# Packed attention with two expert layers on one core: urgencies from backward plans, and six units without moves within SBUF

## The chip, the cores and the metric

One core of one Trainium2 chip runs one launch. The time is device microseconds (us) from one execution; a kernel's time is the median of its runs. TensorE (PE) multiplies, VectorE (DVE), ScalarE (ACT) and GpSimd (POOL) work on vectors, and SyncE (SP) issues nearly all DMAs. On-chip data lies in SBUF; products come out in banks of PSUM.

## The reference

There are 8 batches of 8 heads, 576 positions, 64 elements a head, and 32 packed positions. All is float32 (the weights are laid out as 64-bit floats).

```
p_packed = softmax(p k^T / 8) v          # 32 x 64 a head
att      = softmax(q p_packed^T / 8) p_packed
x   = att as 4608 x 512
h   = x w_in;  s = h softmax(h);  x = layernorm(s) g_ln w_out     # 512 -> 1024 -> 512
out = relu(x moe2_w_in)^2 moe2_w_out                              # 512 -> 2048 -> 512
```

## The kernel before

The kernel writes no instruction at once. Each step is entered in a plan (`plan.op`, `plan.either`) with an engine or several, an estimated duration, an urgency, and the tiles that it reads and writes. `Plan.order` then simulates the five queues (TensorE, ScalarE, GpSimd, VectorE, and one for DMAs): whenever an engine is free it takes the ready step of least urgency number. `Plan.emit` writes the instructions in the order so found, and each engine executes its own in that order. A step waits in its engine's queue until its semaphores come, and all behind it waits too. DMAs are issued from SP in the order of the plan.

**Urgencies.** They are hand-set times: a unit of attention gets `att_at(n)`, with the constants `QA`, `GA`, `UN` and others for single steps; a tile of the first expert layer gets `T0 + DT * i`, and so on for weights and the second layer.

**Attention.** There are 16 units of four heads (`pack` and `unpack`), two to a batch. `pack` loads k (`kr`) and q (`qr`), transposes them on VectorE in blocks of 32 into `kT` (L537, L540) and `qT` (L548), computes the first scores (`s1`), their maximum (`mx`, `nmx`), exp (`e1`, L575), its transposes on TensorE (L588), the packed values (`ppp`, L602; `pp`, L608), and their transposes into `ppq`. `unpack` computes the second scores (`s2`) from `ppq` and q, transposes them (`a`, L637), does the softmax over 32 positions on VectorE, GpSimd and ScalarE, and leaves `aT`; it also multiplies the packed values by w_in (`pg`, L648) into the tile `G`. Line L373 issues the DMAs, L386 is the rounded copy of `hi_op`, L389 the subtraction of `lo_op`.

The scores of a unit contract over 64 elements of each head. In the transposed layout the elements lie in two halves `e` of 32 across four heads. The function `pairs` moves a transposed tile by four DMAs within SBUF (`k2`, `q2`), so that two heads stand in 128 partitions with whole contractions; `pair_mm` (L478) then makes two products of 64 columns of the array each. An `early` unit (n < `NK`, which is 4) does this for q but not for k: its first scores contract the two halves one after the other over the whole array (L560) with the operand `pb`, in which each head has its own columns.

**Buffers.** A ring of n buffers gives the tile n places earlier in the same ring to the next one, after all its uses. k and q share the ring `raw` (`RAW` = 1), `kT`, `qT` and `e1` the ring `tmp` (2), `pr`, `pp` and (other units) `pT` the ring `s` (2), in the order in which they are entered in the plan.

**The first expert layer.** Its tiles of 128 tokens (`h_tile`, 36 of them) need `G` and `aT` of both units of a batch; from the second batch on each operand is split into a high and a low part (`ah`, `al`), the low one by a subtraction (`ALO` names the engine). After softmax and layer norm the tile is transposed (`ptv`) and multiplied by w_out (`y_stage`, `py`). `decode` turns the 64-bit weights into float32; `SIN` and `SOUT` say which engine restores the signs of w_in and w_out (L422 and L423 on VectorE, or L426 and L428 on ScalarE with L430 on VectorE). The second layer (`z_group`, `o_products`) follows and computes seven products of blocks where eight would be plain.

Of the kernel before, what the change touches and what calls it, by code (L numbers as in the profile page):

```python
# [90 lines left out]
class Plan:  # L91

    WINDOW = 3413.0

    @staticmethod
# [21 lines left out]
    def either(self, engines, urgency, fn, r=(), w=(), lag=0, claim=(), port=False):  # L120
# [24 lines left out]
        deps.discard(i)  # L145
        self.ops.append(Op(engines, urgency, fn, lag, bufs, deps, port))

    def order(self):
        ops = self.ops
        users = [[] for _ in ops]  # L150
        left = [len(o.deps) for o in ops]
        able = [[] for _ in range(5)]
# [39 lines left out]
        def take(e, t):  # L192
            nonlocal port
            while not busy[e] and able[e]:
                _, i = heapq.heappop(able[e])
                o = ops[i]
                if o.engine is not None:
                    continue
                o.engine = e
                busy[e] = True  # L200
                order.append(i)
                if e == POOL or e == DVE and o.port:
                    port = self.span = max(t, port) + o.engines[e]
                else:
                    self.span = pe_end(t, o.engines[e]) if e == PE else t + o.engines[e]
                heapq.heappush(events, (self.span, i, "free"))
                heapq.heappush(events, (self.span + o.lag, i, "done"))

# [25 lines left out]
        assert len(order) == len(ops), "the plan is stuck"  # L234
        return order

    def emit(self):
        with self.tc.manual_schedule():
            for i in self.order():
                self.ops[i].fn(self.ops[i].engine)  # L240
            for s in reversed(list(self.stacks.values())):
                s.close()
# [3 lines left out]
def kernel(  # L246
# [36 lines left out]
    KJ = (S + P - 1) // P  # L283
    SH = S // 2
    ST = 256
    AB, GB, RAW, TMP, VR, ET = 4, 4, 1, 2, 1, 1
    QA, GA, HA, TR, UN = 55.91, 149.84, 34.68, -39.93, -11.33
    NK = 4
    WD, WDS, WIS = 99.51, 175.52, 17.0
    GSC = (POOL,)  # L290
    SIN, SOUT = DVE, ACT
    GX = 1
    SUB, KLO, ALO = (POOL,), (DVE,), (DVE,)
    ZSIN, OSIN = DVE, DVE
    SN, FN, LATE = 5.72, -26.79, 3090.0
    YB, ZL, OL, GL0, GL1, GL2, PS, CS = 197.3, 148.71, 20.73, 15.29, 13.31, 32.6, 1.04, 186.23
    NST = NT // ST
    HN = 384
    NSZ = NT // (2 * HN)
# [58 lines left out]
    def c_prod(n, cols, whole):  # L358
        return c_mm(n * (4 if whole else 3), cols, whole)

    def c_dve(cols, fast=False):
        return 66 + (0.525 if fast else 1.045) * cols
# [107 lines left out]
    rows = [min(P, S - j * P) for j in range(KJ)]  # L470

    pbz = [ab.tile([P, 2, HG, 32] if i == 0 else [P, 2, 2, 32], F32, f"pbz{i}") for i in range(3)]
    PAIR = 4 * (0.4336 * SH + 6)

    def pair_mm(ps, lhs, rhs, cs):

        for e in range(2):
            nc.tensor.matmul(ps()[64 * e:64 * e + 64, :SH], cols(lhs, e), cols(rhs, e)[:, cs], start=True, stop=True)  # L478
# [13 lines left out]
    def pack(at, b, g):  # L492
# [43 lines left out]
        for e in range(2):  # L536
# [10 lines left out]
        qT = ab.tile([P, 2, NB, T], F32, "qT", tag="tmp", bufs=TMP)  # L547
        plan.op(DVE, c_dve(2 * S), at + QA, lambda: nc.vector.transpose(  # L548
            out=qT().rearrange("p e n t -> p n e t"), in_=qr().rearrange("p n (e i) -> p n e i", e=2)), r=[qr], w=[qT])
        qs = pairs(at + QA + 1, qT, "q2")  # L550

        mx = ab.tile([P, 2], F32, "mx")
        s1 = []
# [44 lines left out]
        def pp_mm():  # L598
            for j in range(KJ):
                m = rows[j]  # L600
                for e in range(2):
                    nc.tensor.matmul(  # L602
                        ppp()[64 * e:64 * e + 64, :2 * D].rearrange("p (h m i) -> p h m i", h=2, m=2),
                        eT()[:m, j, 64 * e:64 * e + 64], vr()[:m, 2 * e:2 * e + 2, j, :].rearrange("p m (h i) -> p h m i", h=2), start=j == 0, stop=j == KJ - 1)
        plan.op(PE, KJ * 267, at + 10, pp_mm, r=[eT, vr], w=[ppp])

        pp = ab.tile([P, 2, P], F32, "pp", tag="s", bufs=2)
        plan.op(DVE, c_dve(256) + 60, at + 12, lambda: nc.vector.scalar_tensor_tensor(  # L608
# [7 lines left out]
        def pp_tr():  # L616
            for e in range(2):
# [2 lines left out]
        ppq = ab.tile([P, 2, 64], F32, "ppq", bufs=2)  # L620
        hi_op(at + 12, P, ppq,
              lambda: ptp()[:, :2 * (P + 64)].rearrange("p (e n) -> p e n", e=2)[:, :, :64], [ptp], [ppq])
        return ppq, qs

    g_tiles, a_tiles = {}, {}

    def unpack(at, b, g, packed):
        ppq, qs = packed

        a = ab.tile([P, NB, NP], F32, "a1", bufs=1)  # L630
        for hf in range(2):
            s2 = bank("s2")

            def s2_mm(s2=s2, cs=slice(hf * SH, (hf + 1) * SH)):
                pair_mm(s2, ppq, qs, cs)
            plan.op(PE, PAIR, at, s2_mm, r=[ppq, qs], w=[s2])
            plan.op(DVE, c_dve(SH), at + 1, lambda s2=s2, bs=slice(hf * NB // 2, (hf + 1) * NB // 2): nc.vector.transpose(  # L637
                out=a()[:, bs, :], in_=s2()[:, :SH].rearrange("p (n t) -> p n t", t=T)), r=[s2], w=[a])

        gt = m1.tile([P, 1, F1], F32, "G", bufs=GB) if b < GX else m1.tile([P, 2, F1], F32R, "G", bufs=GB)  # L640
        for f in range(F1 // 512):
            pg = bank("pg")
            fs = slice(f * 512, (f + 1) * 512)

            def g_mm(pg=pg, fs=fs):
                for e in range(2):
                    es = slice(64 * e, 64 * e + 64)
                    nc.tensor.matmul(pg()[es, :], ppq()[:, e], wi[2 * g + e]()[:, fs], start=True, stop=True)  # L648
            plan.op(PE, 885, at + GA, g_mm, r=[ppq, wi[2 * g], wi[2 * g + 1]], w=[pg], claim=[gt])
            hi_op(at + GA + 1, 512, lambda fs=fs: gt()[:, 0, fs], pg, [pg], [gt])  # L650
            if b >= GX:
                lo_op(at + GA + 1, 512, lambda fs=fs: gt()[:, 1, fs], pg, lambda fs=fs: gt()[:, 0, fs], [pg, gt], [gt], (DVE,))
        g_tiles[b, g] = gt
        m2_ = ab.tile([P, NB], F32, "m2_")
        plan.op(DVE, c_dve(S), at + 2, lambda: nc.vector.tensor_reduce(
            out=m2_(), in_=a(), axis=AX.X, op=ALU.max), r=[a], w=[m2_])
        plan.either({e: on(S, e)[e] if e == DVE else 1110 for e in SUB}, at + 3, lambda e: vec[e].tensor_tensor(
            a(), a(), m2_().unsqueeze(2).to_broadcast([P, NB, NP]), op=ALU.subtract), r=[a, m2_], w=[a])
        plan.op(ACT, c_act(S, sbuf=True), at + 4, lambda: nc.scalar.activation(a(), a(), AF.Exp, scale=scale), r=[a], w=[a])
        d2 = ab.tile([P, NB], F32, "d2")  # L660
        plan.op(DVE, c_dve(S), at + 5, lambda: nc.vector.tensor_reduce(
            out=d2(), in_=a(), axis=AX.X, op=ALU.add), r=[a], w=[d2])
        plan.op(DVE, 85, at + 5, lambda: nc.vector.tensor_scalar(d2(), d2(), 1e-9, None, op0=ALU.add), r=[d2], w=[d2])
        plan.op(DVE, 180, at + 5, lambda: nc.vector.reciprocal(d2(), d2()), r=[d2], w=[d2])
        plan.op(POOL, 1110, at + 6, lambda: nc.gpsimd.tensor_tensor(
            a(), a(), d2().unsqueeze(2).to_broadcast([P, NB, NP]), op=ALU.mult), r=[a, d2], w=[a])
        aT = m1.tile([P, NB, T], F32, "aT", bufs=AB)
        plan.op(DVE, c_dve(S), at + 7, lambda: nc.vector.transpose(out=aT(), in_=a()), r=[a], w=[aT])
        a_tiles[b, g] = aT
# [144 lines left out]
    g_mark = [[[plan.mark("g") for _ in range(4)] for b in range(4)] for st in range(NSZ)]  # L814


    T0, DT = 127.57, 23.948
    PD0, PD = 111.2, 23.139
    UD, UA, U1 = 25.541, 213.28, -45.68
    WI, WO, WOD, YL = 162.35, 266.68, 65.988, 3.36  # L820
    units = [(b, g) for b in range(B) for g in range(NG)]
    att_at = lambda n: U1 * n if n < NG else T0 - UA + UD * (n - NG)
    packed = {}
# [332 lines left out]
            o_products(at, st)  # L1156

    second()
    plan.emit()


# [28 lines left out]
```

## Time and profile before

| | us |
|---|---|
| median of 3 runs (lowest, highest) | 1263.37 (1262.45, 1266.02) |
| profiled execution | 1262.49 |
| its span, first to last instruction | 1260.4 |
| TensorE busy in the span | 1205.5 |
| VectorE, ScalarE, GpSimd busy | 906.0, 789.7, 171.7 |

A share of busy time over the span is a mean over stages with different limits, so the stages have to be looked at one by one. Matmuls overlap, and their ends are modelled in the profile: of two neighbours the distance of their starts tells more than the duration.

### The profile page before, as it was taken

What the parts mean: (1) busy time and instruction counts of PE and PEld (TensorE: products, weight loads), DVE (VectorE), ACT (ScalarE), POOL (GpSimd) and SP (SyncE); (2) the same over time, 40 slices, a digit from 0 to 9 for tenths busy, and PEclk for the clock granted to TensorE, in tenths of its full rate; (3) what the DMA queues carried; (4) which work ended last, traced back from release to release, by engine and by line L of the source; (5) the groups of instructions that cost most, each with busy time, mean ns of one, the idle gap of its engine ahead of it and who ended that gap; (6) DMA issues with size and microseconds to landing.
All of it is one profiled execution on the core that took longest, in us unless ns stands there. A gap on an engine that the chain in (4) does not pass through costs nothing.

```text
span 1260.4 us, 23326 instructions
## 1 busy us (share of the span) xinstructions
PE 1205.5 (96%) x8332; PEld 1101.2 (87%) x8332; DVE 906.0 (72%) x1817; ACT 789.7 (63%) x1678; POOL 171.7 (14%) x181
## 2 busy tenths in 40 slices
PE   4668999999999999999999999999899999999998
PEld 2336788877888789999999999999899999999998
DVE  5888678787766874455686868662678787878786
ACT  2476577666776666577777878777554555555453
POOL 1364323333332340000000000000000000000000
PEclk9878999999999999999999999999899999999999
DMA  8856756776756649465767676753986535343501
GB/s 214 224 154 168 204 156 174 216 197 170 205 150 193 171 125 329 157 200 197 242 199 248 205 249 206 230 166 130 351 341 210 157 121 158 112 151 110 171 32 51
DMA packets 185240, 234.60 MB, mean 186 GB/s; under 512 B 24356, under 2 KB 148772, under 8 KB 184356
## 3 DMA queue, kind: packets, MB, share of 16 engines
q1 hardware_dynamic: 184260, 232.33, 60.2%
q8 instruction: 65, 1.06, 0.4%
q10 hardware_dynamic: 864, 0.79, 0.2%
q14 instruction: 51, 0.42, 0.1%
HBM read 130.55 MB, written 85.98 MB: 172 GB/s over the span
## 4 chain that ended last, share of the span: by engine, by line
PE 78%; DMA 5%; DVE 4%; ACT 3%; issue 1%; SPq 1%; ACTq 0%; DVEq 0%
PE px L404 9%; PE px L406 8%; PE px L405 8%; PE ph L719 7%; PE py L404 5%; PE py L405 5%; PE py L406 5%; PE pa L404 5%; PE pa L406 5%; PE pa L405 5%; PE ptv L762 3%; PE s L478 2%; PE pg L648 2%; PE pz L406 2%; PE pz L405 2%; PE pz L404 2%
## 5 line engine op out<-in xcount | busy, mean ns | idle before, releaser
L386 ACT CAST cb<-ga 128x384 fp32r<-128x384 f32 x336 | 168.0, 513 | 168.3 <-PE px L406 70.9
L389 DVE TENSOR_TENSOR cb<-ga,cb 128x384 fp32r<-128x384 f32 x336 | 180.5, 555 | 60.8 <-ACT cb L386 59.5
L404 PE MATMUL py<-v,wo 128*128 128x256 f32 x576 | 169.3, 294 | 0.0
L405 PE MATMUL py<-v,wo 128*128 128x256 f32 x576 | 163.5, 284 | 0.0
L406 PE MATMUL py<-v,wo 128*128 128x256 f32 x576 | 163.2, 283 | 0.0
L404 PE MATMUL px<-oi,cb 128*128 128x256 f32 x504 | 142.8, 283 | 2.9 <-ACT cb L386 2.9
L406 PE MATMUL px<-oi,cb 128*128 128x256 f32 x504 | 142.5, 283 | 0.8 <-DVE cb L389 0.8
L405 PE MATMUL px<-oi,cb 128*128 128x256 f32 x504 | 142.4, 282 | 0.0
L404 PE MATMUL pa<-oi,cb 128*128 128x256 f32 x504 | 141.4, 281 | 0.0
L406 PE MATMUL pa<-oi,cb 128*128 128x256 f32 x504 | 141.0, 280 | 0.0
L405 PE MATMUL pa<-oi,cb 128*128 128x256 f32 x504 | 141.0, 280 | 0.0
L404 PE MATMUL px<-y,zi 128*128 128x384 f32 x384 | 130.3, 339 | 1.8 <-ACT gw L963 1.7
L405 PE MATMUL px<-y,zi 128*128 128x384 f32 x384 | 129.6, 337 | 0.4 <-DVE y L389 0.3
L406 PE MATMUL px<-y,zi 128*128 128x384 f32 x384 | 129.3, 337 | 0.0
L404 PEld LDWEIGHTS py<-v,wo 128*128 128x128 f32 x576 | 110.6, 192 | 9.1 <-issue 7.8
L967 DVE TENSOR_TENSOR gw<-pz,gw 128x384 f32<-128x384 f32 x96 | 53.2, 554 | 81.1 <-PE pz L406 66.2
L405 PEld LDWEIGHTS py<-v,wo 128*128 128x128 f32 x576 | 110.8, 192 | 0.7
L406 PEld LDWEIGHTS py<-v,wo 128*128 128x128 f32 x576 | 110.6, 192 | 0.0
L907 DVE TENSOR_TENSOR ga<-ga 128x384 f32<-128x384 f32 x192 | 99.7, 552 | 2.6 <-DMA ga<-g_dram 1.9
L404 PEld LDWEIGHTS px<-oi,cb 128*128 128x128 f32 x504 | 96.4, 191 | 3.2 <-ACT cb L386 3.2
L406 PEld LDWEIGHTS px<-oi,cb 128*128 128x128 f32 x504 | 96.5, 191 | 1.1 <-DVE cb L389 1.1
L975 ACT ACTIVATE gw<-gw 128x384 f32<-128x384 f32 x115 | 60.2, 523 | 57.5 <-DVE gw L967 57.1
(180 smaller groups left out, 2990.8 us busy)
## 6 DMA issues: line engine op xcount, KB each, us to landing
g_dram<-gw SPq DMA_DIRECT2D x192, 192.0 KB
ga<-g_dram SPq DMA_DIRECT2D x96, 384.0 KB
zi<-z_dram SPq DMA_DIRECT2D x28, 512.0 KB
oi<-o_dram SPq DMA_DIRECT2D x24, 512.0 KB
kr<-in_k_dram SPq DMA_DIRECT2D x16, 576.0 KB
qr<-in_q_dram SPq DMA_DIRECT2D x16, 576.0 KB
q<-qT SPq DMA_DIRECT2D x64, 144.0 KB
y_dram<-ysb SPq DMA_DIRECT2D x72, 128.0 KB
```

What stands on the lines that cost most here:

```text
L386: plan.op(ACT, c_act(cols, sbuf=r[0].pool not in (psm, psh, pso)), at, lambda: nc.scalar.copy(out_(), in_()), r=r, w=w)
L389: plan.either(on(cols, *engines), at, lambda e: vec[e].tensor_tensor(out_(), in_(), hi_().bitcast(F32), op=ALU.subtract), r=r, w=w, port=i ...
L404: nc.tensor.matmul(ps, lh, rh, start=first, stop=False, skip_group_check=onto)
L405: nc.tensor.matmul(ps, lh, rl, start=False, stop=False, skip_group_check=onto)
L406: nc.tensor.matmul(ps, ll, rh, start=False, stop=last, skip_group_check=onto)
L478: nc.tensor.matmul(ps()[64 * e:64 * e + 64, :SH], cols(lhs, e), cols(rhs, e)[:, cs], start=True, stop=True)
L648: nc.tensor.matmul(pg()[es, :], ppq()[:, e], wi[2 * g + e]()[:, fs], start=True, stop=True)
L719: nc.tensor.matmul(ph()[:, fs], al[l]()[:, g], g_tiles[b, g]()[:, r, fs], start=ends[0] and g == 0 and t == 0, stop=ends[1] and g == NG - ...
L762: nc.tensor.transpose(pt()[:, c * P:(c + 1) * P], e()[:, (4 * t + c) * P:(4 * t + c + 1) * P], ident)
L907: plan.op(DVE, c_dve(cols), at, lambda: nc.vector.tensor_tensor(out_(), in0(), in1(), op=op), r=r, w=w, port=True)
L967: plan.op(DVE, c_dve(HN), when(p, SN), lambda: nc.vector.tensor_tensor(t(), ps()[:, :HN], t(), op=ALU.add), r=[t, ps], w=[t])
L975: nc.scalar.activation(t(), t(), AF.Relu)
```

## The change

Each run of the planner is followed by one backwards: it goes through the planned steps from the end, with the engines and PSUM banks that the forward plan gave them, and gives each step the time that is left from its start to the end as its new urgency. Then it plans forward again; this is done eight times (`PASSES`). The hand-set urgencies remain as the start of the first plan, with other constants.

Six units are early instead of four, and an early unit has no moves of q either: the second scores take `qT` as it is and a new operand `ppT`, which VectorE transposes from `pp`, in two products over the whole array. Besides, `RAW` becomes 2, `SOUT` becomes VectorE, `ALO` becomes GpSimd, and three estimates of durations on TensorE rise.

```diff
+    def reset(self):
+        for o in self.ops:
+            o.engine = None
+            for b in o.bufs:
+                b.slot = None
+                if b.ring:
+                    b.ring.free, b.ring.queue = list(range(b.ring.bufs)), []
+
+    def backward(self):
+        ops, ends = self.ops, self.ends
+        deps = [set(o.deps) for o in ops]
+        slots = {}
...
+        for bufs in slots.values():
+            bufs.sort(key=lambda b: ends[b.touched[0]])
+            for a, b in zip(bufs, bufs[1:]):
+                deps[b.touched[0]].update(a.touched)
...
+                if what == "ready":
+                    heapq.heappush(able[e], (-ends[i], i))
+                    continue
...
+            for e in (PE, ACT, POOL, DVE, DMA):
+                if not busy[e] and able[e]:
+                    _, i = heapq.heappop(able[e])
+                    busy[e] = True
+                    starts[i] = now + ops[i].engines[e]
+                    if e == POOL or e == DVE and ops[i].port:
+                        port = starts[i] = max(now, port) + ops[i].engines[e]
+                    heapq.heappush(events, (starts[i], i, "free"))
+        end = max(starts)
+        for o, t in zip(ops, starts):
+            o.urgency = round((end - t) / 1e3, 6)
...
-    def emit(self):
+    def emit(self, passes):
+        order = self.order()
+        for _ in range(passes):
+            self.backward()
+            order = self.order()
...
-    AB, GB, RAW, TMP, VR, ET = 4, 4, 1, 2, 1, 1
-    QA, GA, HA, TR, UN = 55.91, 149.84, 34.68, -39.93, -11.33
-    NK = 4
-    WD, WDS, WIS = 99.51, 175.52, 17.0
+    AB, GB, RAW, TMP, VR, ET = 4, 4, 2, 2, 1, 1
+    QA, GA, HA, TR, UN = 55.91, 149.84, -4.64, -48.02, -12.62
+    NK = 6
+    WD, WDS, WIS = 98.4, 177.845, 17.0
...
-    SIN, SOUT = DVE, ACT
+    SIN, SOUT = DVE, DVE
...
-    SUB, KLO, ALO = (POOL,), (DVE,), (DVE,)
+    PASSES = 8
+    SUB, KLO, ALO = (POOL,), (DVE,), (POOL,)
...
-    PAIR = 4 * (0.4336 * SH + 6)
+    PAIR = 4 * (0.4336 * SH + 6) + 85
...
-        qs = pairs(at + QA + 1, qT, "q2")
+        qs = qT if early else pairs(at + QA + 1, qT, "q2")
...
-        plan.op(PE, KJ * 267, at + 10, pp_mm, r=[eT, vr], w=[ppp])
+        plan.op(PE, KJ * 280 + 60, at + 10, pp_mm, r=[eT, vr], w=[ppp])
...
-        return ppq, qs
+        if not early:
+            return ppq, ppq, qs
+        ppT = ab.tile([P, 2, HG, 32], F32, "ppT", tag="s", bufs=2)
+        plan.op(DVE, c_dve(256), at + 12, lambda: nc.vector.transpose(
+            out=ppT().rearrange("p h (e m) n -> p e h (m n)", e=2), in_=pp().rearrange("p e (h x) -> p e h x", h=2)), r=[pp], w=[ppT])
+        return ppq, ppT, qs
...
-        ppq, qs = packed
+        ppq, ppl, qs = packed
+        early = NG * b + g < NK
...
-                pair_mm(s2, ppq, qs, cs)
-            plan.op(PE, PAIR, at, s2_mm, r=[ppq, qs], w=[s2])
+                if early:
+                    for h in range(2):
+                        nc.tensor.matmul(s2()[:, :SH], cols(ppl, h), cols(qs, h)[:, cs], start=h == 0, stop=h == 1)
+                else:
+                    pair_mm(s2, ppl, qs, cs)
+            plan.op(PE, c_prod(2, SH, True) if early else PAIR, at, s2_mm, r=[ppl, qs], w=[s2])
...
-            plan.op(PE, 885, at + GA, g_mm, r=[ppq, wi[2 * g], wi[2 * g + 1]], w=[pg], claim=[gt])
+            plan.op(PE, 957, at + GA, g_mm, r=[ppq, wi[2 * g], wi[2 * g + 1]], w=[pg], claim=[gt])
...
-    plan.emit()
+    plan.emit(PASSES)
```

The other constants that differ only shift the first plan's urgencies (`HA`, `TR`, `UN`, `SN`, `ZL`, `DT`, `PD0`, `PD`, `UA`, `U1`, `WI`, `WOD`, `YL`).

## Rows read from the trace of the kernel before

**Rows 1.** stages: length, busy us (instructions) of each engine, granted clock, DMA share, GB/s

```profile
0.00:50.00 50.00, 23.01 (x96) 12.85 (x97) 31.63 (x59) 13.10 (x30) 9.49 (x25) 0.90 0.94 225
50.00:110.00 60.00, 43.05 (x193) 23.17 (x191) 55.43 (x85) 42.55 (x72) 33.61 (x21) 0.86 0.57 159
110.00:1260.40 1150.40, 1139.49 (x8044) 1065.20 (x8044) 818.91 (x1675) 734.06 (x1577) 128.62 (x135) 1.00 0.60 186
...
800.00:1000.00 200.00, 196.37 (x1379) 195.63 (x1379) 129.34 (x262) 122.40 (x260) 0.00 (x0) 0.98 0.65 224
```

**Rows 2.** what TensorE waited for before 50 us: sum, times, longest, us

```profile
PE pt L588 <- ACT e L575: 6.9, 2, 4.7
PE ptp L618 <- DVE pp L608: 5.1, 2, 3.9
```

**Rows 3.** the same from 50 to 110 us

```profile
PE pt L588 <- ACT e L575: 8.9, 3, 7.0
PE ph L696 <- DVE aT L668: 2.5, 1, 2.5
```

**Rows 4.** TensorE in order of time: start, us, work, [idle before it]

```profile
27.11 3.33 PE L560 MATMUL s<-kT,pbz 128*128 128x288 f32 x8
...
45.28 3.17 PE L478 MATMUL s<-q,ppq 128*64 128x288 f32 x8 [3.47 <-issue]
...
51.02 2.10 PE L560 MATMUL s<-kT,pbz 128*128 128x288 f32 x8
...
128.27 1.19 PE L478 MATMUL s<-k,pbz 128*64 128x288 f32 x8
```

**Rows 5.** SP's DMA issues in order of time

```profile
40.31 1.74 SPq L373 DMA_DIRECT2D q<-qT  x3
```

**Rows 6.** VectorE in order of time, same columns

```profile
12.53 0.46 DVE L564 TENSOR_REDUCE mx<-s 128x1 f32<-128x288 f32 x1
13.86 1.38 DVE L548 STREAM_TRANSPOSE qT<-qr 128x1152 f32<-128x1152 f32 x1 [0.88 <-DMA qr<-in_q_dram]
15.16 0.17 DVE L570 TENSOR_SCALAR nmx<-mx 128x1 f32<-128x1 f32 x1
...
21.29 1.23 DVE L435 SCALAR_TENSOR_TENSOR wraw<-wraw 128x1024 f32<-128x1024 uint32 x1
24.86 0.74 DVE L422 TENSOR_SCALAR wi<-wi 128x1024 int32<-128x1024 int32 x1 [2.34 <-ACT wi L419]
25.51 0.70 DVE L537 STREAM_TRANSPOSE kT<-kr 128x512 f32<-128x512 f32 x1
26.14 0.43 DVE L608 SCALAR_TENSOR_TENSOR pp<-ppp,rs,mask 128x256 f32<-128x256 f32 x1
...
110.66 0.10 DVE L745 TENSOR_TENSOR den<-den,vs 128x1 f32<-128x1 f32 x1
...
115.59 0.71 DVE L537 STREAM_TRANSPOSE kT<-kr 128x512 f32<-128x512 f32 x1
```

**Rows 7.** groups of VectorE's instructions to 110 us: xcount, busy us, mean ns

```profile
L435 DVE SCALAR_TENSOR_TENSOR wraw<-wraw 128x1024 f32<-128x1024 uint32 x8 | 11.3, 1418 | 0.1
...
L537 DVE STREAM_TRANSPOSE kT<-kr 128x512 f32<-128x512 f32 x10 | 6.7, 687 | 1.8 <-DMA kr<-in_k_dram 1.8
L430 DVE SCALAR_TENSOR_TENSOR wx<-wx,wraw 128x1024 int32<-128x1024 int32 x4 | 6.0, 1493 | 0.0
...
L423 DVE SCALAR_TENSOR_TENSOR wi<-wraw,wi 128x1024 int32<-128x1024 int32 x4 | 4.8, 1201 | 0.0
...
L422 DVE TENSOR_SCALAR wi<-wi 128x1024 int32<-128x1024 int32 x4 | 2.8, 693 | 7.6 <-ACT wi L419 7.6
...
L745 DVE TENSOR_TENSOR den<-den,vs 128x1 f32<-128x1 f32 x3 | 2.4, 784 | 0.0
...
L389 DVE TENSOR_TENSOR al<-aT,ah 128x64 fp32r<-128x64 f32 x1 | 1.9, 1900 | 0.0
```

**Rows 8.** groups of GpSimd's instructions from 110 to 500 us

```profile
L801 POOL TENSOR_TENSOR wx<-wx 128x128 f32<-128x128 f32 x29 | 13.5, 467 | 2.6 <-DVE wx L801 0.5
```

More of the change, by code (lines that the diff above doesn't have):

```diff
@@ L146, in either @@
         self.ops.append(Op(engines, urgency, fn, lag, bufs, deps, port))
+    def reset(self):
[9 more added lines that the diff above has]
+        slots = {}
+        for b in dict.fromkeys(b for o in ops for b in o.bufs if b.slot is not None):
+            slots.setdefault((b.ring, b.slot), []).append(b)
+        for bufs in slots.values():
+            bufs.sort(key=lambda b: ends[b.touched[0]])
+            for a, b in zip(bufs, bufs[1:]):
+                deps[b.touched[0]].update(a.touched)
+        left = [0] * len(ops)
+        for i, d in enumerate(deps):
+            d.discard(i)
+            for j in d:
+                left[j] += 1
+        able = [[] for _ in range(5)]
+        busy = [False] * 5
+        free, starts = [0.0] * len(ops), [0.0] * len(ops)
+        port = 0.0
+        events = [(0.0, i, "ready") for i in range(len(ops)) if not left[i]]
+        heapq.heapify(events)
+        while events:
+            now = events[0][0]
+            while events and events[0][0] <= now:
+                t, i, what = heapq.heappop(events)
+                e = ops[i].engine
+                if what == "ready":
+                    heapq.heappush(able[e], (-ends[i], i))
+                    continue
+                busy[e] = False
+                for j in sorted(deps[i]):
+                    left[j] -= 1
+                    free[j] = max(free[j], t + self.hop(ops[j].engine, e) + ops[j].lag)
+                    if not left[j]:
+                        heapq.heappush(events, (free[j], j, "ready"))
+            for e in (PE, ACT, POOL, DVE, DMA):
[9 more added lines that the diff above has]
+            o.urgency = round((end - t) / 1e3, 6)
@@ L148, in order @@
     def order(self):
         ops = self.ops
+        self.reset()
+        self.ends = [0.0] * len(ops)
         users = [[] for _ in ops]
@@ L205, in take @@
                     self.span = pe_end(t, o.engines[e]) if e == PE else t + o.engines[e]
+                self.ends[i] = self.span
                 heapq.heappush(events, (self.span, i, "free"))
@@ L235, in order @@
         return order
-    def emit(self):
+    def emit(self, passes):
[3 more added lines that the diff above has]
+            order = self.order()
         with self.tc.manual_schedule():
-            for i in self.order():
+            for i in order:
                 self.ops[i].fn(self.ops[i].engine)
@@ L285 @@
     ST = 256
[L286 to L289 removed]
+    AB, GB, RAW, TMP, VR, ET = 4, 4, 2, 2, 1, 1
+    QA, GA, HA, TR, UN = 55.91, 149.84, -4.64, -48.02, -12.62
+    NK = 6
+    WD, WDS, WIS = 98.4, 177.845, 17.0
     GSC = (POOL,)
[L291 removed]
+    SIN, SOUT = DVE, DVE
     GX = 1
[L293 removed]
+    PASSES = 8
+    SUB, KLO, ALO = (POOL,), (DVE,), (POOL,)
     ZSIN, OSIN = DVE, DVE
[L295 to L296 removed]
+    SN, FN, LATE = 10.55, -26.79, 3090.0
+    YB, ZL, OL, GL0, GL1, GL2, PS, CS = 197.3, 185.94, 20.73, 15.29, 13.31, 32.6, 1.04, 186.23
     NST = NT // ST
@@ L814 @@
     g_mark = [[[plan.mark("g") for _ in range(4)] for b in range(4)] for st in range(NSZ)]
[L817 to L820, printed above, removed]
+    T0, DT = 127.57, 23.129
+    PD0, PD = 116.78, 25.885
+    UD, UA, U1 = 25.541, 206.59, -43.17
+    WI, WO, WOD, YL = 131.61, 266.68, 64.814, 3.23
     units = [(b, g) for b in range(B) for g in range(NG)]
```

## The prediction

> **What bounds the kernel now.** I read the busy time by stages first [rows 1]. From 110 us to the end TensorE is busy for 1139.49 of 1150.4 us at a granted clock of 1.00: nothing but less TensorE work can shorten that stretch, apart from 3.6 us idle between 800 and 1000. Before 110 us it is busy for 23.01 + 43.05 = 66.06 of 110 us, so 43.9 of the 54.9 idle us of the whole span (1260.4 - 1205.5) lie there, and the granted clock is 0.90 and 0.86. A new order of work can only gain in this ramp. Next I asked who holds TensorE up there. Before 50 us it is one unit's own chain (scores, exp, transposes, packed values) [rows 2]; the DMA share is 0.94, so loads and moves within SBUF compete. From 50 to 110 us it waits 8.9 us for exp and 2.5 us for the transposed weights [rows 3], but behind both stands VectorE: 55.43 busy of 60 us. So the ramp has two limits: data up to about 50 us, VectorE after that. This separates the parts of the change: one that only frees DMA counts early, one that adds VectorE work costs late, one that adds TensorE work costs in full after 110 us.
>
> **The moves that go.** A unit's transposed queries are moved within SBUF by 4 DMAs; for the first six units these go, for units 4 and 5 those of the keys too: 6 x 4 + 2 x 4 = 32 moves of 144 KB. Unit 1's second scores start at 45.28 after 3.47 us of idle time [rows 4], and SP issued its last three moves from 40.31 to 42.05 [rows 5]. That wait goes: -3.5.
>
> **Whole products.** Without the move the two heads of a pair are not side by side, and the score product takes the full array. One unit's scores took 2.10 us whole (at 51.02) and 1.19 us in pairs (at 128.27) [rows 4]: +0.9 a unit and kind. The second scores of six units and the first scores of two change: 8 x 0.9 = 7.2 us of TensorE work. I count unit 1's 0.9 in its chain. Of the rest, units 0, 2 and 3 run where TensorE has idle time to hide theirs (if that cover is gone, +2.7); units 4 and 5 fall about where it is full, 4 x 0.9 = +3.6. Bounds 0 and 6.3.
>
> **Buffers.** RAW = 2 lets unit 0's queries load at once and not after its key transposes. Now VectorE's queue holds nmx (15.16) behind qT (13.86), which waits for that load, though the second maximum ended at 12.99 [rows 6]: -2.2, and at least 0. Likewise pp of unit 0 stands behind unit 1's key transpose (25.51): TensorE waited 3.9 us for it, pp itself takes 0.43 [rows 2, 6]: -3.5; or 0, if VectorE then stands at the weight decode (24.86) instead.
>
> Against this the diff makes a wait that no line names. With no move, qT is read by the second scores, and it lies in the ring "tmp" of two buffers, whose next but one user, after e1, is the next unit's kT. So the keys of unit n+1 can't be transposed before the second scores of unit n are done; behind them on VectorE stands whatever the plan put there, and TensorE's next first scores wait too. A second one like it: ppT joins the ring "s" of two, so p of the next unit loads only after pp is used up, and that DMA can hold SP's queue. Unit 0 after both gains: pp at 26.14 - 5.7 = 20.4, about 1.5 us to the packed operand (0.97 us to the next product on TensorE, then one copy), scores whole in 3.3 us as at 27.11, key transposes 1.6 us: unit 1's first scores at 26.8 against 27.11 [rows 4, 6]. The ring eats what the buffers gave; -0.3 is left. Early chain: -0.3 - 3.5 + 0.9 = -2.9.
>
> **VectorE's work in the ramp.** SOUT on VectorE replaces one instruction of 1.493 by two of 0.693 and 1.201 for each of four weight chunks [rows 7]: 4 x 0.40 = +1.6; it frees ScalarE, which isn't the limit. The extra transpose ppT has 256 columns; 512 take 0.687 [rows 7], so 0.34 to 0.69 each; I take 0.4, and 4 units in the ramp: +1.6. Together +3.2.
>
> **ALO.** The subtraction for the low parts of aT goes to GpSimd: no instruction has this form there yet; the nearest, 128x128, takes 0.467 [rows 8], against 1.900 for the one on VectorE in the ramp [rows 7]. Why 1.9 for 64 columns? VectorE's instructions with two SBUF operands grow when GpSimd works: den takes 0.784 on the mean in the ramp and 0.10 at 110.66 [rows 6, 7]. The Trainium skill speaks against moving more work there: SBUF — State Buffer, "Who interferes with whom", says that GpSimd and VectorE share a port pair as an exclusive lock, so that the loser blocks fully. The stretched den agrees with it. By that rule some 70 new GpSimd instructions would make VectorE wait up to 70 x 0.467 = 33 us, an estimate; after 110 us VectorE has the idle time for it (1150.4 - 818.91 [rows 1]), so I put 0 on the path.
>
> **The new order.** Urgencies no longer come from hand-set linear times but from the plan itself, run backwards eight times: an instruction with a long tail behind it goes first. What can that regain from 50 to 110 us? All 60 - 43.05 = 16.95 us of idle TensorE at most, nothing at least. VectorE is nearly full, so I size it by VectorE's time: 4.57 us idle, and what GpSimd stretched: den 3 x (0.784 - 0.10) = 2.05, al 1.9, L435 8 x (1.418 - 1.23) = 1.5 [rows 6, 7]. That makes 10.0, less the 3.2 of new work: -6.8. This is the least certain term, the order being nowhere in the trace. In the turn at 800 to 1000 us a new order can save 3.6 or cost as much; I take 0.
>
> **Sum:** -2.9 (chain) + 3.6 (whole products) - 6.8 (order, VectorE's additions included) = -6.1. Against the profiled execution's 1262.49 (span 1260.4 and 2.1 around it; the median of the runs is 1263.37, 0.9 more) that is 1256.4; I say 1256.
>
> **Rivals.** (a) *The order regains nearly all the idle time*: -16.95 - 2.9 + 3.6 = -16.3, 1246. For it: the exp that holds TensorE for up to 7.0 us [rows 3] is late only through VectorE's queue. Against: VectorE's 55.43 of 60 us.
> (b) *The ramp stays as long*: VectorE's additions eat the regained time, and only the chain and the products count: -2.9 + 3.6 = +0.7, to +3.9 with the 3.2: 1263 to 1266, no change. For it: data limits the first 50 us, and VectorE is full after.
> (c) *The units run one after the other and this sets the ramp*, slower: the ring binds unit n+1's keys to unit n's second scores. In the trace unit 1 takes from 25.51 to 48.45, 22.9 us [rows 4, 6]; unit 5's keys start at 115.59, four steps of 22.5. So from about 22.5 us a unit on, the ring decides, and each us more makes the sixth unit 4 us later. At 25 us it is 10 late; with half hidden by other products, +5 + 3.6 = 1271.
> (d) The moves don't matter: unit 1 waits elsewhere. That changes 3.5 and is inside the range.
>
> **Chances.** Forecast 0.42, (a) 0.17, (b) 0.20 with (d), (c) 0.21. About 0.3% (3.8 us) is what can be told from no change. Faster takes the forecast and (a): 0.59; within 0.3%: 0.19; slower: 0.22. The forecast's own range is 1250 to 1260; for 8 in 10 it reaches to (a) and nearly to (c): 1244 to 1270, which holds the bounds of the products and buffers.
>
> **What would show it.** No q moves before the seventh unit and no wait before unit 1's second scores; whole scores of 2.1 us a unit six times. TensorE's idle time to 110 us falls from 43.9 to about 34, and the stretch behind keeps its clock of 1.00. VectorE's idle time and its stretched instructions shrink between 50 and 110 us. Wrong: kT waiting for the second scores with TensorE idle; a busy sum grown by more than 7.2; new idle time past 110 us, where a load or a GpSimd result comes late in the new order; or a second turn at 900 us that costs more than 3.6.

## The result and the profile after

The changed kernel takes 1272.94 us (median of 11 runs, 1268.19 to 1279.08) against 1265.47 for the kernel before beside it (1261.21 to 1269.27): the ratio is 1.0059 [1.0042, 1.0075], so it is slower, by 7.5 us. The forecast was 1256.0 us with a range of 1244 to 1270. The execution that was profiled is the slowest of the eleven, 1279.08 us with a span of 1277.2; the median run's span is 1270.9.

Busy time of each engine in the stages of [rows 1], then granted clock, DMA share and GB/s:

```profile
0.00:50.00 50.00, 20.93 (x84) 12.52 (x84) 32.25 (x51) 12.55 (x28) 11.60 (x26) 0.76 0.87 201
50.00:110.00 60.00, 48.02 (x173) 23.64 (x174) 56.53 (x92) 31.82 (x62) 38.86 (x22) 0.86 0.45 131
110.00:1277.20 1167.20, 1146.39 (x8076) 1068.94 (x8074) 811.29 (x1632) 727.41 (x1574) 152.22 (x196) 1.00 0.58 182
```

Idle time of TensorE up to 110 us is 29.1 + 12.0 = 41.1 us against 43.9 in [rows 1]: 2.8 less, where about 10 less was forecast. Behind it stand 1167.20 - 1146.39 = 20.8 us against 10.9: nearly 10 more. And TensorE is busy for 1215.3 us in all against 1205.5, 9.8 more. So of the 16.8 us by which the two spans differ, 9.8 are busy and 7.0 idle time. The medians lie only 7.5 us apart: more than half of these 16.8 come with the execution that was profiled, so the two shares can't be carried over to the 7.5. What TensorE waited for up to 110 us, to hold beside [rows 2, 3] (sum, times, longest, us):

```profile
PE pt L653 <- ACT e L640: 20.5, 3, 8.1
PE s L625 <- DVE kT L602: 11.1, 1, 11.1
PE s L625 <- DVE pbz L582: 4.5, 2, 2.9
...
PE s L708 <- DVE ppT L691: 0.9, 1, 0.9
```

The wait for exp grew from 6.9 + 8.9 to 20.5 us, and the first scores start late. Both can be followed in order of time, with the rows that answer to [rows 4], behind the first scores of the kernel before:

```profile
7.31 4.18 PE L560 MATMUL s<-kT,pbz 128*128 128x288 f32 x8 [7.31 <-DVE kT L537]
```

```profile
11.08 4.18 PE L625 MATMUL s<-kT,pbz 128*128 128x288 f32 x8 [11.08 <-DVE kT L602]
21.67 1.30 PE L653 MATMUL pt<-ident,e 128*128 128x128 f32 x5 [6.41 <-ACT e L640]
...
28.92 4.18 PE L708 MATMUL s<-qT,ppT 128*128 128x288 f32 x8 [0.89 <-DVE ppT L691]
...
45.23 1.39 PE L653 MATMUL pt<-ident,e 128*128 128x128 f32 x5 [8.12 <-ACT e L640]
...
55.47 2.10 PE L708 MATMUL s<-qT,ppT 128*128 128x288 f32 x8
...
69.17 1.39 PE L653 MATMUL pt<-ident,e 128*128 128x128 f32 x5 [5.98 <-ACT e L640]
```

Unit 0 starts at 11.08, where before it was 7.31. The second scores of a unit are eight whole products (L708). Unit 1's have no wait of their own, but start at 55.47, where before it was 45.28: their predecessors are late. Part of the reason is the order of the loads on SP; the line behind them is from the kernel before:

```profile
1.25 0.57 SPq L438 DMA_DIRECT2D wraw<-in_moe_w_in_dram  x1
...
2.32 0.43 SPq L438 DMA_DIRECT2D kr<-in_k_dram  x1
2.79 1.86 SPq L438 DMA_DIRECT2D wraw<-in_moe_w_in_dram  x4
4.70 0.61 SPq L438 DMA_DIRECT2D vr<-in_v_dram  x1
5.36 5.17 SPq L438 DMA_DIRECT2D wraw<-in_moe_w_in_dram  x3
```

```profile
1.85 0.43 SPq L373 DMA_DIRECT2D kr<-in_k_dram  x1
```

Eight of the eleven loads in this stretch are weights, 256 KB each (the load left out is p). VectorE, waiting for unit 0's keys, starts their transposes 7.9 us after the issue at 2.32; before, the keys were issued at 1.85 ahead of any weights, and it took 4.6 us. ScalarE then stands at the first step of the weight decode (L484), and behind it in its queue stands exp (L640): the waits (sum, times, longest), first in the changed kernel and then before, and two rows in order of time (the profile puts the first row's idle time down to the load of the queries, but the step reads weights):

```profile
ACT wi L484 <- DMA wraw<-in_moe_w_in_dram: 22.5, 3, 10.9
```

```profile
ACT wi L419 <- DMA wraw<-in_moe_w_in_dram: 5.7, 3, 2.2
```

```profile
19.92 1.13 ACT L484 ACTIVATE wi<-wraw 128x1024 f32<-128x1024 f32 x1 [4.32 <-DMA qr<-in_q_dram]
20.95 0.48 ACT L640 ACTIVATE e<-s,nmx 128x288 f32<-128x288 f32 x1
```

The units also follow one another more strictly than before. The second scores of units 0 to 3 start at 28.92, 55.47, 80.11 and 105.32, some 25 us apart, and the next unit's keys are transposed only behind each of them, as rival (c) had it:

```profile
33.37 0.71 DVE L602 STREAM_TRANSPOSE kT<-kr 128x512 f32<-128x512 f32 x1
...
58.16 0.70 DVE L602 STREAM_TRANSPOSE kT<-kr 128x512 f32<-128x512 f32 x1
...
85.16 0.71 DVE L602 STREAM_TRANSPOSE kT<-kr 128x512 f32<-128x512 f32 x1
```

The first scores of units 2 and 3 then wait for pbz, which VectorE transposes beside the keys: the 4.5 us in the list above.

### The profile page after: what moved, and what is told of

It is laid out like the page before. It is cut to its first block, busy times and chain, and to the rows that moved or that the text cites. A ratio compares the mean times of both kernels' runs of the same rounds, so it can differ in the third digit from the quotient of the medians.

```text
span 1277.2 us, 23283 instructions
## 1 busy us (share of the span) xinstructions
PE 1215.3 (95%) x8332; PEld 1105.1 (87%) x8332; DVE 900.1 (70%) x1773; ACT 771.8 (60%) x1663; POOL 202.7 (16%) x243
## 4 chain that ended last, share of the span: by engine, by line
PE 70%; DVE 9%; DMA 9%; ACT 4%; issue 4%; SPq 2%; POOL 1%; DVEq 0%; ACTq 0%
PE px L469 8%; PE px L471 8%; PE px L470 8%; PE ph L794 5%; PE pa L469 5%; PE pa L471 5%; PE pa L470 5%; PE py L469 4%; PE py L470 4%; PE py L471 4%; PE ptv L837 2%; PE pz L469 2%; PE pz L471 2%; SPq L438 2%; PE pz L470 2%
```

## The experiments

Three theories were open. *The products*: the first six units have 7.2 us more work on TensorE, and that is the loss. *The ramp's order*: exp behind late weights on ScalarE, with the loads of the weights first, keeps the ramp long, so the new order gains nothing. *The order past the ramp*: what the plan wins in the ramp it loses later. A fourth, the prediction's rival (c), is that the two rings bind the units to one another. All kernels ran in five rounds; ratios are to the kernel before beside them.

**One part at a time.** The kernel before with nothing but the new order:

```diff
+    def reset(self):
...
+    def backward(self):
...
-    plan.emit()
+    plan.emit(8)
```

> The kernel before with nothing new but the eight backward plans. If the new order is what costs (weight work goes ahead of the units' own chain in queues that run in order), this alone is slower than before by 4 to 10 us, its first scores start later than 7.3 us, and idle time of TensorE past 110 us grows from 10.9 to nearly 20 us. If the whole products and their rings cost, the order alone is no slower than before: 1257 to 1266 us.

Measured: 1264.22 us, 0.9994 [0.9981, 1.0008]. The order by itself is worth nothing that can be told. The stages say how (window, busy time of PE, PEld, DVE, ACT and POOL, clock, DMA share), with the last row from the kernel before:

```profile
50.00:110.00 60.00, 48.53 (x245) 26.55 (x245) 55.98 (x91) 45.23 (x80) 37.72 (x24) 0.89 0.60 168
110.00:130.00 20.00, 16.90 (x104) 13.36 (x103) 11.81 (x25) 8.27 (x23) 5.05 (x5) 0.94 0.65 182
130.00:500.00 370.00, 362.32 (x2536) 293.39 (x2536) 266.76 (x555) 241.48 (x537) 115.88 (x123) 0.99 0.61 171
```

```profile
130.00:500.00 370.00, 369.15 (x2616) 304.71 (x2615) 272.03 (x559) 249.92 (x552) 118.03 (x125) 1.00 0.66 189
```

From 50 to 110 us the idle time fell from 17.0 to 11.5 us, as the prediction wanted. But 110 to 130 us has 3.1 (0.6 before) and 130 to 500 us has 370 - 362.32 = 7.7, where the kernel before had 370 - 369.15 = 0.9. Up to 130 us the order gains 2.4 us of idle time, and between 130 and 1000 us it loses 6.3; in this execution TensorE is busy 0.8 less. Behind 130 us no single wait stands out: the longest kind up to 500 us has 2.9 us in three waits, and the runs don't show which step of the order makes them.

The changed kernel with the hand-set urgencies (it keeps the new constants):

```diff
-    PASSES = 8
+    PASSES = 0
```

> The changed kernel without a backward plan: its six units of whole scores, its buffers, its engines and its constants in the order of the hand-set urgencies. If the order costs, this is 4 to 10 us faster than the changed kernel, near 1265 us. If the whole products and the rings cost, it is as slow as the changed kernel, 1270 to 1276 us, and TensorE's busy sum stays 7 us above that of before. Its constants were not set for this order, so a slower time than both says little.

Measured: 1276.69 us, 1.0088 [1.0070, 1.0106]. The rest of the change costs without the order too, though its constants were set for a planned order.

The changed kernel with the moves kept in all units and all second scores in pairs (the new order, RAW, SOUT, ALO and the constants stay):

```diff
-    NK = 6
+    NK = 4
...
-        qs = qT if early else pairs(at + QA + 1, qT, "q2")
+        qs = pairs(at + QA + 1, qT, "q2")
...
-        if not early:
-            return ppq, ppq, qs
+        return ppq, ppq, qs
...
-        early = NG * b + g < NK
+        early = False
```

> The changed kernel with four early units whose q is moved within SBUF again (no ppT, no whole second scores); backward plans, buffers and engines stay. If whole products and rings cost, TensorE's busy sum falls by 6 to 7 us and the time by 5 to 9, to about 1265 us. If the order costs, the time stays within 4 us of the changed kernel, since the weight work still goes first.

Measured: 1266.18 us, 1.0012 [0.9998, 1.0027]. With these two the loss divides: order -0.8 us, buffers, SOUT, ALO and constants +2.3 (the two intervals overlap), whole units (1.0059 - 1.0012) x 1264.6 = +5.9. In these three plans it is with the whole units that no change becomes a loss. But each plan has an order of its own, and the runs at other prices below show that this division doesn't hold in other orders.

More buffers in the two rings that the whole units' operands live in:

```diff
-    AB, GB, RAW, TMP, VR, ET = 4, 4, 2, 2, 1, 1
+    AB, GB, RAW, TMP, VR, ET = 4, 4, 2, 3, 1, 1
...
-            pr = ab.tile([P, D], F32, "pr", tag="s", bufs=2)
+            pr = ab.tile([P, D], F32, "pr", tag="s", bufs=4)
```

The other tiles of the ring "s" get the same count.

> The changed kernel with three buffers in the ring tmp and four in the ring s, planned anew. If the wait of the next unit's keys for the second scores sets the ramp (rival c), the ramp shortens by 5 us or more and the waits of first scores for pbz (4.5 us) go; time about 1266 us. If late loads in front of the queues set it, the time stays within 4 us of the changed kernel.

Measured: 1274.29 us, 1.0075 [1.0056, 1.0095], no better than the changed kernel. Yet the rings did hold the units up. The whole second scores of the six units, with the first and last start in us, first in the changed kernel and then here, and two stages here:

```profile
L708 PE MATMUL s<-qT,ppT x48: 403/406/820, 28.9 to 186.5; 128*128 128x288 f32 x48
```

```profile
L708 PE MATMUL s<-qT,ppT x48: 406/406/817, 27.2 to 110.0; 128*128 128x288 f32 x48
```

```profile
0.00:50.00 50.00, 26.72 (x108) 16.11 (x108) 32.17 (x62) 13.65 (x33) 11.33 (x26) 0.92 0.94 227
50.00:110.00 60.00, 47.01 (x219) 25.54 (x218) 55.33 (x110) 25.76 (x62) 29.86 (x20) 0.86 0.57 165
```

All six units have come to their second scores by 110 us instead of 186, and the idle time up to there is 36.3 us instead of 41.1. The gain is lost again right behind: 110 to 130 us has 6.0 us idle (0.9 in the changed kernel). In this plan, then, freeing the units doesn't end the kernel sooner.

**Is it TensorE's work?** In the order of the changed kernel, one of the two products of each whole score is left out: in the second scores of units 0 to 5 and the first scores of units 4 and 5 (half_all), in the second scores of units 0 to 3 alone (half_first), in both scores of units 4 and 5 alone (half_late). The plan still charges both, so the order stays:

```diff
-                    for e in range(2):
-                        nc.tensor.matmul(ps()[:, :SH], cols(pb, e), cols(ks, e)[:, cs], start=e == 0, stop=e == 1)
+                    for e in range(1 if 4 <= n < 6 else 2):
+                        nc.tensor.matmul(ps()[:, :SH], cols(pb, e), cols(ks, e)[:, cs], start=e == 0, stop=e == 1 or 4 <= n < 6)
...
-                    for h in range(2):
-                        nc.tensor.matmul(s2()[:, :SH], cols(ppl, h), cols(qs, h)[:, cs], start=h == 0, stop=h == 1)
+                    for h in range(1 if 0 <= NG * b + g < 6 else 2):
+                        nc.tensor.matmul(s2()[:, :SH], cols(ppl, h), cols(qs, h)[:, cs], start=h == 0, stop=h == 1 or 0 <= NG * b + g < 6)
```

> The changed kernel in its own order, with one of the two products left out in the second scores of all six early units and in the first scores of units 4 and 5 (half of the contraction is missing): 8 times 0.97 = 7.8 us of TensorE work less, all waits as they are. If the products' work on TensorE is what the change costs, this is 6 to 8 us faster than the changed kernel, near 1265 us. If the rings or the order around them cost, it is less than 3 us faster.

> The same, with the second scores of units 0 to 3 alone halved, 3.9 us less work in the ramp. By the prediction's step (TensorE's idle time in the ramp hides them) the time stays within 1.5 us of the changed kernel. If the ramp's products lie on the chain of the units, 4 us or more are gained.

> The same, with both scores of units 4 and 5 alone halved, 3.9 us less work where TensorE is full. By the prediction's step these count in full: 3 to 4 us faster than the changed kernel, about 1269 us. If TensorE has slack there too (its idle time past 110 us has grown), less than 1.5 us.

Measured: half_all 1270.61 us, 1.0043 [1.0027, 1.0059]; half_first 1268.43, 1.0042 [1.0020, 1.0065]; half_late 1268.36, 1.0042 [1.0027, 1.0058]. Half of eight whole scores at about 2 us each is some 8 us of TensorE work; leaving it out gave 2 us, and so did leaving out either half of it; the intervals still touch that of the changed kernel. The theory of the products fell in its plain form: in this order most of their work is not what sets the time.

**The loads' order.** The plan charges a load its bytes at 358 a nanosecond. [rows 1] show 225 GB/s moved in the first 50 us. With that price for the loads of keys, queries, values and the first layer's weights, and all else as in the changed kernel:

```diff
-    def dma(at, out_, in_, nbytes, r=(), w=(), spare=0, queue=nc.sync):
+    def dma(at, out_, in_, nbytes, r=(), w=(), spare=0, queue=nc.sync, rate=358.0):
...
-        plan.op(DMA, max(430.0, nbytes / 358.0), at, lambda: queue.dma_start(out=out_(), in_=in_()), r=r, w=w, lag=2200 + spare)
+        plan.op(DMA, max(430.0, nbytes / rate), at, lambda: queue.dma_start(out=out_(), in_=in_()), r=r, w=w, lag=2200 + spare)
...
-        dma(at, kr, lambda: k[b, hs].rearrange("h (t n) d -> (h t) n d", n=NB), 4 * P * NB * D, w=[kr])
+        dma(at, kr, lambda: k[b, hs].rearrange("h (t n) d -> (h t) n d", n=NB), 4 * P * NB * D, w=[kr], rate=225.0)
```

> The changed kernel with one estimate in the plan changed: the loads of k, q, v and of the first layer's weights are planned at 225 bytes a ns (what the first 50 us moved before) and not 358. If the order loses because ScalarE and VectorE stand at weights that land later than planned, the exp's 20.5 us of waits in the ramp shrink by 5 or more and the time falls by 3 to 8 us. If the products cost, it stays within 2 us of the changed kernel; a changed plan alone may move it by some us either way.

Measured: 1263.42 us, 0.9989 [0.9979, 0.9999]. All whole products are there, and the loss is gone. Waits up to 110 us, and the second scores of unit 1:

```profile
PE ptp L683 <- DVE pp L673: 8.6, 4, 4.0
PE s L625 <- DVE kT L602: 8.3, 1, 8.3
...
PE pt L653 <- ACT e L640: 5.5, 2, 4.0
```

```profile
8.33 3.72 PE L625 MATMUL s<-kT,pbz 128*128 128x288 f32 x8 [8.33 <-DVE kT L602]
...
42.62 3.65 PE L708 MATMUL s<-qT,ppT 128*128 128x288 f32 x8 [2.09 <-DVE ppT L691]
```

The first scores start at 8.33, the wait for exp is 5.5 us, and unit 1's second scores start at 42.62, about where the prediction's chain had put them (some 2.9 us before 45.28). The stages up to 110 us:

```profile
0.00:50.00 50.00, 28.14 (x104) 16.85 (x105) 32.33 (x61) 12.72 (x30) 11.35 (x27) 0.83 0.79 204
50.00:110.00 60.00, 47.08 (x210) 26.26 (x209) 58.11 (x99) 33.04 (x69) 33.80 (x22) 0.89 0.46 143
```

The idle time is 21.9 + 12.9 = 34.8 us, 9.1 less than before and just what the prediction forecast for the ramp (about 34). The kernel is faster than the one before by about 0.1% only: of its 1262.0 - 1210.9 = 51.1 us of idle time 16.3 lie behind 110 us, 5.4 more than before, and TensorE is busy 5.4 us more.

**Is it exp behind the weights?** The finished order of the changed kernel is kept, but the maxima, nmx and exp of units 0 to 3 are taken out and put right behind the last step that they need:

```diff
+        for i in self.first:
+            order.remove(i)
+            place = {j: n for n, j in enumerate(order)}
+            order.insert(max((place[d] for d in self.ops[i].deps), default=-1) + 1, i)
```

> The changed kernel's own order with the maxima, nmx and exp of units 0 to 3 put right behind what they need, so that on VectorE and ScalarE they stand in front of the weight work; nothing else moves, no tile or product differs. If the order costs because exp stands behind weights that land late, TensorE's 20.5 us of waits for exp in the ramp fall below 10 and the time falls by 4 to 9 us, to about 1266 us. If the loss lies past the ramp, or comes from products and rings, it falls by less than 2 us.

Measured: 1276.13 us, 1.0081 [1.0059, 1.0103]. The wait was cured and nothing was won:

```profile
PE ppp L678 <- ACT eT L456: 9.1, 2, 4.8
PE s L630 <- DVE kT L607: 8.3, 1, 8.3
...
PE pt L664 <- ACT e L649: 4.6, 3, 1.6
PE ppp L678 <- DMA vr<-in_v_dram: 4.1, 1, 4.1
```

The wait for exp fell from 20.5 to 4.6 us; in its place TensorE waits 9.1 us for the next step on ScalarE, eT, and 4.1 for the values. The theory that this one wait sets the ramp fell.

In the same way, but with nothing moved except unit 0's loads, which go ahead of all weights (the same two lines stand behind the loads of p and q; the first piece of the values goes along):

```diff
         dma(at, kr, lambda: k[b, hs].rearrange("h (t n) d -> (h t) n d", n=NB), 4 * P * NB * D, w=[kr])
+        if n == 0:
+            plan.first.insert(0, len(plan.ops) - 1)
```

> The changed kernel's own order with unit 0's loads of p, k and q and the first piece of v issued in front of all weight loads. If the late start of the ramp (first scores at 11.1 us, 7.3 before) is part of the loss, the first scores start near 7 us and the time falls by 2 to 4 us. If exp behind late weights sets the ramp, the gain is lost again at that wait and the time falls by less than 2 us.

Measured: 1275.70 us, 1.0090 [1.0070, 1.0111]. The first scores start at 7.4 us, and the gain ends at the next wait, that for exp:

```profile
PE pt L667 <- ACT e L654: 25.8, 3, 12.3
```

The whole chain of units 0 to 3 on TensorE, ScalarE and VectorE put as early as its operands allow:

```diff
+        if unit < 4:
+            plan.first += [i for i in range(begin, len(plan.ops)) if set(plan.ops[i].engines) <= {PE, ACT, DVE}]
```

> The changed kernel's own order with the whole chain of units 0 to 3 (first scores, maximum, exp, transposes, packed values, operands) put right behind what it needs on TensorE, VectorE and ScalarE. In exp_first the wait moved one step down, to the copies of the transposes. If the units' chain behind late weights is the loss, the ramp's idle time now falls by 5 us or more and the time to about 1266 us. If the weight work is as urgent as the chain, it only moves the wait once more and the time stays within 3 us of the changed kernel.

Measured: 1306.37 us, 1.0334 [1.0319, 1.0349], 42 us slower than before. VectorE now stands at the chain's own steps (busy 21.0 of the first 50 us, 32.3 in the changed kernel), so the other work in its queue is late, and TensorE waits for aT:

```profile
PE ph L783 <- DVE aT L755: 21.9, 2, 11.9
```

The in-order queues have two users that are about equally urgent, the chain of the packed values and the rest (the weights, the second softmax that leaves aT); pulling one forward pushed the other back.

**How much is one draw?** Other numbers of passes (PASSES = 7, 9), other prices for the loads (340 and 500), and the price of 225 with the moves kept (load_price's and moves_kept's edits together):

> The changed kernel with seven backward plans in place of eight: another order from the same rule. If one order of this rule is as good as the next, the time stays within 2 us of the changed kernel. If the loss is that of this one order, it lands elsewhere, between 1262 and 1275 us, with other waits in the ramp.

> The same with nine. Together with seven and eight it shows how far orders of one rule lie apart: within 2 us if the rule sets the time, by 5 us or more if the single order does.

> The changed kernel with the loads planned at 340 bytes a ns instead of 358: a control for load_price, since any number changes the order. If a truer price of loads is what gave 9 us, this one, hardly truer, stays within 3 us of 1273 us. If any other order does as well, it falls to 1268 us or less.

> The same at 500 bytes a ns, further from what the ramp moves. If the price matters, no better than the changed kernel, 1272 us or more, with ScalarE waiting longer for w_in in the ramp. If orders only scatter, it may land on either side.

> The kernel of moves_kept with loads planned at 225 bytes a ns. If the whole products cost their 7 us of TensorE work whatever the order, this is 5 to 7 us faster than load_price, near 1257 us. If their cost was that of the order planned around them, it stays within 3 us of load_price, 1261 to 1266 us.

Measured: passes7 1273.71 us, 1.0074 [1.0053, 1.0094]; passes9 1274.49, 1.0072 [1.0048, 1.0096]; price340 1274.72, 1.0088 [1.0072, 1.0104]; price500 1280.22, 1.0124 [1.0106, 1.0142]; moves_225 1281.26, 1.0135 [1.0120, 1.0151]. One pass more or less changes nothing that can be told; the plan's inputs do. They do it in no simple way: at 358 the whole units are 5.9 us slower than the moves, at 225 they are (1.0135 - 0.9989) x 1264.6 = 18 us faster. A truer price is no cure by itself. What a part costs depends on the order that it is in by more than the part's own work.

**The whole units in the hand-set order.** The kernel before with the whole units alone:

```diff
-    NK = 4
+    NK = 6
...
-        qs = pairs(at + QA + 1, qT, "q2")
+        qs = qT if early else pairs(at + QA + 1, qT, "q2")
...
+        ppT = ab.tile([P, 2, HG, 32], F32, "ppT", tag="s", bufs=2)
...
+            plan.op(PE, c_prod(2, SH, True) if early else PAIR, at, s2_mm, r=[ppl, qs], w=[s2])
```

> The kernel before with only the six whole units (no moves of q, ppT, whole second scores, first scores of units 4 and 5 whole), in the order of the hand-set urgencies, with its own constants and buffers. If the whole units cost by themselves, 1269 to 1273 us, TensorE's busy sum 6 to 7 us above before. If they cost only in the orders that backward plans find around them, 1262 to 1267 us: their work then hides in the ramp.

Measured: 1279.09 us, 1.0111 [1.0088, 1.0134], +14.0 us. Stages:

```profile
0.00:50.00 50.00, 27.59 (x100) 14.98 (x101) 32.00 (x53) 13.30 (x31) 11.35 (x26) 0.97 0.76 190
...
110.00:130.00 20.00, 20.00 (x144) 16.14 (x142) 9.78 (x27) 10.46 (x23) 2.56 (x3) 0.95 0.33 103
130.00:500.00 370.00, 362.47 (x2535) 297.31 (x2534) 271.86 (x554) 237.66 (x530) 122.71 (x128) 1.00 0.62 176
```

Up to 130 us TensorE's idle time fell from 44.6 to 37.5 us, so the ramp took the added work into its gaps, as the prediction said, though by then 404 products had run where it was 421 before. But 130 to 1000 us has 7.1 us more of it, and TensorE is busy 13.8 us more in all: 10.6 more for scores (61.0 against 50.4), 3.8 more for pg (37.3 against 33.5), 0.6 less for the rest. The sum of the three is the 13.7 us between the two spans.

The order alone again, but with the plan's urgencies only for what it puts before 130 us, and the hand-set ones behind:

```diff
+        for o, u, t in zip(self.ops, hand, list(self.ends)):
+            o.urgency = o.urgency - 1e4 if t < 130e3 else u
+        order = self.order()
```

> The kernel of order_only with the backward order kept only for steps planned before 130 us; all later ones follow the hand-set urgencies again. If backward orders gain in the ramp and lose past it (order_only: idle time to 130 us 42.2 against 44.6, from 130 to 1000 us 13.1 against 6.7), idle time past 130 us falls back to 7 and the time is 1256 to 1261 us, below before. If the loss past the ramp is a debt of what the ramp did first, it stays at 1263 to 1266 us.

Measured: 1269.76 us, 1.0030 [1.0015, 1.0046]. If the plan's urgencies past the ramp were what costs there, this kernel would have kept the ramp's gain and been faster. It keeps 17.3 us idle between 130 and 1000 us. So that theory fell too; that the ramp puts work off which is then missing fits, and so does a hand-set order that doesn't suit this ramp. These two are not told apart.

## Why the prediction was wrong

**The order: the step that failed.** "The new order" was -6.8 us, by VectorE's time from 50 to 110 us: 10.0 gained, less 3.2 of new work. order_only, which has none of the new work, measured -0.8, with zero inside its interval. TensorE's idle time from 50 to 110 us did fall there, by 5.5 us, and VectorE's fell from 4.57 to 3.5 in the changed kernel. The mistake was to take what the ramp gets back for what the span gets back. load_price shows it best: it has the forecast ramp (34.8 us idle) and not the forecast time. 130 to 1000 us, which has 6.7 us idle before, was given no term but the turn's 3.6, taken as 0, and the planned orders show from 10.9 (moves_kept) to 21.3 us (chain_first) there.

**Whole products: mis-sized.** The unit prices were right where the clock is at its upper level: 2.10 us whole, and ppT 0.43 for the 0.4 taken; unit 0's scores took 4.18. "Units 0, 2 and 3 run where TensorE has idle time to hide theirs" was right for the ramp and wrong for the end: +3.6 and 0.9 in the chain were counted; whole_only measured +14.0, the changed kernel +5.9 against moves_kept. Full price, 7.2, would have been nearer to the first and no further from the second; in the orders planned at a price of 225 the sign turned round (-18).

**The early chain.** The wait for the moves went, as forecast. "-2.9" didn't come: unit 1's second scores start 10.2 us later than before, because nothing in the sum had the order push the first keys' landing or exp. In load_price's order they come 2.7 us earlier than before, so what failed here is the order's part, not the moves'. That RAW = 2 brings 2.2 was not tried alone.

**Rivals.** (a) fell with order_only. (b), the ramp as long as before, is what the ramp shows: 41.1 us idle against 43.9; its price lacked the loss behind the ramp. (c) had the side, nearly the number (1271) and its own condition, 25 us a unit: the changed kernel's units lie 26.6, 24.6 and 25.2 us apart, and the next keys stand behind each unit's second scores. But this isn't shown to be what costs: rings freed the units and took 1274.29 us, in a plan of its own, and whole_only, whose fourth unit has its second scores at 97.36 where the kernel before has them at 98.02, took 1279.09. So the near number of (c) is luck as far as these runs show. (d) was not decided. The forecast named three signs that came, "kT waiting for the second scores with TensorE idle" (4.5 us), "new idle time past 110 us" and "a busy sum grown by more than 7.2", and gave the last two no price.

**ALO and SOUT.** Most of ALO's instructions took 0.46 us for 128 columns and 0.32 for 64, as estimated (0.48 and 0.39 on the mean); a cost on the path isn't to be told from the +2.3 us of four edits together.

**What stays open.** What makes one order good, and so what the 7.5 us are made of: the same kernel takes 1263.4 to 1280.2 us by the price of its loads in the plan alone. No kernel beat the one before by more than about 0.1%; load_price comes nearest. TensorE's clock in the ramp doesn't sort the times either: in the first 50 us it is 0.97 in whole_only (1279.09 us), 0.92 in rings (1274.29) and 0.83 in load_price (1263.42). Not tried: ALO, SOUT or RAW alone, and the whole units with hand-set due times made for them.

## What to carry to other kernels

Idle time of the bound engine in one stage is not a cover that is free: work hidden in it and waits cured in it can come back as idle time further on, so take added work at its full price and read an order by all its stages. Before the result of a new order is put down to one of its parts, run neighbours of the order (another price, another count of passes): here they lie further apart than the part is worth. And a cured wait counts only when the next one in the chain is shown to be shorter too.

## What the hardware showed that was not expected

A VectorE instruction with one input can be stretched by GpSimd too: in the changed kernel a decode step that takes 0.69 us alone took 2.73, while GpSimd worked from 52.16 to 54.55. VectorE and then GpSimd in order of time:

```profile
52.37 2.73 DVE L487 TENSOR_SCALAR wx<-wx 128x1024 int32<-128x1024 int32 x1
```

```profile
52.16 2.39 POOL L503 TENSOR_TENSOR wi<-wi,wraw 128x1024 f32<-128x1024 f32 x1 [5.27 <-DVE wraw L500]
```

It ended at 55.10, 0.55 us behind GpSimd's end, so it hardly ran beside it. A second one, from 76.03 to 77.47, also ended 0.55 us behind a GpSimd instruction. The Trainium skill, SBUF — State Buffer, "Who interferes with whom", calls the shared port pair an exclusive lock; the trace agrees.

Unit 0's keys, 576 KB, took 7.9 us from issue to their transposes with one load of weights ahead of them and seven issued behind them by 10.5 us; before it was 4.6 us, with no weights ahead and two behind. Which of the loads delays them was not told apart.

The ramp's clock isn't one number: the granted clock of the first 50 us is 0.76 in the changed kernel, 0.90 before, 0.93 in order_only and 0.73 in moves_kept. TensorE's busy time moves with it: order_only and moves_kept have the same products as the kernel before, which is busy for 1205.5 us, and are busy for 1204.8 and 1211.0. Three stretches with whole scores in the changed kernel (columns as in the stages):

```profile
28.90:33.10 4.20, 4.18 (x10) 2.59 (x12) 2.47 (x6) 0.00 (x0) 1.98 (x1) 0.52 1.01 205
55.50:57.50 2.00, 2.00 (x9) 1.30 (x7) 0.86 (x2) 0.00 (x0) 0.00 (x0) 1.00 0.85 219
11.10:15.20 4.10, 4.10 (x8) 2.47 (x8) 1.08 (x3) 0.72 (x1) 0.00 (x0) 1.00 1.05 223
```

Unit 0's second scores ran at about the lower level (0.52, 1.2 GHz) and took 4.18 us; in the 13.6 us before them TensorE had been busy for 4.6. Unit 1's ran at the upper one and took 2.10, behind work without a gap from 50.04 on. But unit 0's first scores, the first work of all, took 4.18 us too, with a granted clock of 1.00 on record; why, the runs don't show.
